# GpSimd makes a slot's last quarter of w2's low parts, and attention's end runs the early table's product and the logits in another order

## The chip, the cores and the metric

The kernel runs on one NeuronCore of a Trainium2 chip. The metric is the device time of one execution, in microseconds (us). The engines are TensorE (PE: matrix products and transposes), VectorE (DVE), ScalarE (ACT), GpSimd (POOL) and SyncE (SP), which only issues transfers. Each works through its own list of instructions in order and waits for the others by semaphores. PE has two clock levels, 1.2 and 2.4 GHz; the profile gives the granted clock as a share of the higher one.

## The reference

Three stages follow each other: attention with a local window and 32 global tokens per head, a layer of 8 experts of which each token takes one, and a dense layer with ELU.

```python
s_ll = np.where(abs(pos[:, None] - pos[None, :]) <= 32, scale * q_l @ k_l.T, -1e9)
a_l = softmax(concat([scale * q_l @ k_g.T, s_ll]))
out_l = a_l @ concat([v_g, v_l])            # 4 batches, 8 heads, 512 local rows of 64
out_g = softmax(scale * q_g @ concat([k_g, k_l]).T) @ concat([v_g, v_l])   # 32 global rows
x = concat([out_g, out_l])                   # 2176 rows of 512
...
logits = x @ w_gate                          # 8 experts
e_idx = argmax(logits)
h = maximum(x[mask] @ w1[e], 0)              # 512 -> 1024
out[mask] = gate_w * eom * (h @ w2[e])       # 1024 -> 512
...
h = x @ w_in                                 # 512 -> 2048
g = where(h > 0, h, exp(minimum(h, 0)) - 1)
return g @ w_out                             # 2048 -> 512
```

## The kernel before

Every large product is made of three products of operands that are split into a high and a low part (x = xh + xo, w = wh + wl): high by high, high by low, low by high. ACT casts the raw weights to the high part (L777), and the low part is raw minus high (L778), by DVE or POOL as the caller says. In the names of the trace, r is a raw weight buffer, w1h, w1l, w2h and w2l are the parts, xh and xo those of the gathered rows, hh and ho those of the hidden rows, h, y, t and tp are banks of PSUM, and misc is the bank that the small results of routing share.

**Attention** runs 16 steps, one per batch and pair of heads, in a software pipeline of 17 turns t. The order of the pieces in a turn is the list PLAN, a string of short names: s0 and s1 are the scores of step t+1, e0 and e1 their maxima and exponentials, pt0 and pt1 the transposes of the probabilities of step t, pc0 and pc1 their copies, pv0 and pv1 the products with the values of step t-1, nm the norm of step t-1 (it makes X, and sends it to the DRAM table x_pre). v1 and v2 are four copies on POOL that build vw, the shifted values of step t, which pv0 and pv1 of the next turn read. Routing follows two steps behind: xt transposes X of step t-2, lm makes its logits in misc, la adds them up in lsum (DVE).

Two slots of expert 0 start on the first three batches alone. Their early table is made in turn 15: ea (L625) counts, eb (L643) is twelve small products that give the two columns of row numbers xidx (DVE, L645), and then two gathers of 128 rows each (L748, an indirect transfer that POOL issues) bring the rows from x_pre to xt. In turn 16, xa transposes them (L798, eight transposes) and makes xh (ACT) and xo (DVE).

**The expert stage** goes through slots of 128 rows. In slot s PE makes the first layer of s in two halves (l1, L811), in between the second layer of s-1 in two halves (l2, L831) and transposes. If the expert of slot s+1 is new, the four quarters of its w1 are split in this slot (L918 and L927 in slot()); if that of slot s is new, the four quarters of its w2 are split (L924, L932, L935). Each of these stands under a branch on a register, as do the slots from 17 on, which run only if the slot count asks for it (L956): an engine that leaves the last slot has to finish what it has there, and then raises the semaphores for the slots that it skips. Here 20 of 26 slots run.

**The dense stage** begins behind it: transposes of the first rows (L990), their split (ACT L992, DVE L993) into the buffer that held the raw w2 of odd slots, the conversion of the dense weights (ACT L1011, POOL L1012), the second layer of the last slot (L831 once more), and then the products of the dense layer (L1041, L1099).

The schedule is written by hand; the order of the calls is the order on each engine. Waits follow from the data and from buffers that are used again, banks of PSUM among them: moe() takes banks that attention has left, in the order in which it asks for them.

Of the kernel before, what the change touches and what calls it, by code (L numbers as in the profile page):

```python
# [44 lines left out]
PLAN = (  # L45
    ("pv0 pv1 pt0 s0 lt pc0 xa e0 rg xt rg2 pt1 gt gu gc gd pump v1 pc1 s1 w1 e1 ld gs lm gpv v2 nm rk bq ea ge "
     "gn eb la", "VAVAVV"),
    ("w1 pv0 ld pt0 s0 rg2 lt xt pv1 pc0 pt1 gt v1 pump gu pc1 rk rg s1 gc gd gs v2 e0 lm nm ea e1 xa gpv ge bq "
     "gn eb la", "AAAAAA"),
    ("pv0 ld pt0 rg2 xt pump ea pv1 pc0 pt1 v1 pc1 v2 lm eb nm la", "AAAAAA"),  # L50
    ("pv0 pv1 nm rg2 xt xa lm la", "AAAAAA"),
)


# [71 lines left out]
class Kern:  # L126
# [7 lines left out]
    def new(self, shape, dt, tag, bufs=1):  # L134
        return (self.home.get(tag) or self.main).tile(shape, dt, tag=tag, name=tag, bufs=bufs)
# [5 lines left out]
    def attention(self):  # L141
        nc, tc, I = self.nc, self.tc, self.i
# [209 lines left out]
        def fetch(t):  # L352
            load_kq(t + 4)
            load_v(t + VB - 1 if t else 16)
            if 3 <= t < 11:
                j, h = divmod(t - 3, 2)
                c = slice(512 * h, 512 * h + 512)
                nc.sync.dma_start(out=self.r1[0][:, j, c], in_=self.w1v[0][:, j, c])
            elif 12 <= t < 16:
                h, j = divmod(t - 12, 2)  # L360
                c = slice(2 * j, 2 * j + 2)
                nc.sync.dma_start(out=self.r2[0][:, h, c], in_=self.w2v[0][:, h, c])
# [7 lines left out]
        for t in range(17):  # L370
# [44 lines left out]
                steps["gs"] = lambda: gscores(g0)  # L415
                steps["ge"] = lambda: gexp(g0)
            steps["ld"] = lambda: fetch(t)
            self.plan = PLAN[0 if t < 2 else 1 if t < 15 else t - 13]
            for x in self.plan[0].split():
                if x in steps:  # L420
                    steps[x]()
# [358 lines left out]
    def split_w1(self, s, h, js=(0, 2)):  # L780
        if s < NSLOT:
            c = slice(512 * h, 512 * h + 512)
            for j in js:
                e = self.nc.gpsimd if (h == (1 if s else 0) and j == 2) else self.nc.vector
                self.split(self.w1h[:, j:j + 2, c], self.w1l[:, j:j + 2, c], self.r1[s % 2][:, j:j + 2, c], e)

    def split_w2(self, s, h, js=(0, 2), engines=None):
# [51 lines left out]
    def moe(self):  # L839
        nc, tc, I = self.nc, self.tc, self.i  # L840
        new = self.new
        SP = mybir.EngineType.SP
        self.hps, self.yps, self.tps = ([self.psum(f"{a}{i}") for i in range(n)] for a, n in (("h", 3), ("y", 1), ("t", 3)))
        self.w2h, self.w2l = (new([128, 2, 4, 512], F32R, a) for a in ("w2h", "w2l"))
        self.r1.append(new([128, 4, 1024], F32, "r11"))
        self.r2.append(new([128, 2, 4, 512], F32, "r21"))
# [68 lines left out]
        def slot(s):  # L915
            n0, n1 = self.nw, self.anew(s + 1)
            l1(s, 0)
            with self.when(n1):  # L918
                self.split_w1(s + 1, 0)
            l2(s - 1, 0)  # L920
            trh(s, 0)
            trx(s + 1)
            self.load_x(s + 4)
            with self.when(n0):  # L924
                self.split_w2(s, 0)
            l1(s, 1)
            with self.when(n1):  # L927
                self.split_w1(s + 1, 1)
            self.load_w1(s + 3)
            l2(s - 1, 1)  # L930
            nc.vector.tensor_copy(self.cur, self.scol[:, s % 3])
            with self.when(n0):  # L932
                self.split_w2(s, 1, (0,), (nc.gpsimd,))
            trh(s, 1)
            with self.when(n0):  # L935
                self.split_w2(s, 1, (2,), (nc.vector,))
            self.load_w2(s + 2)
            self.nw = n1

# [287 lines left out]
```

## Time and profile before

| what | value |
|---|---|
| median of 3 runs | 788.71 us (787.2 to 792.68) |
| the profiled execution | 791.05 us, of which the span from the first to the last instruction is 788.7 us |
| mean granted clock of PE | 0.989 |
| attention | 0 to 129 us |
| expert stage | 129 to 384 us |
| dense stage | 384 to 789 us |

The order of time gives an instruction's start and duration (or of several that follow each other, with their count), and in square brackets how long its engine had been idle before it, and what ended that.

### The profile page before, as it was taken

The page shows a single profiled execution, that of the slowest core. Times are in us where ns is not written, and L with a number is a line of the kernel's source. Part 1 is how long each engine was busy: PE and PEld are TensorE (multiplying, and loading weights), DVE is VectorE, ACT ScalarE, POOL GpSimd, SP SyncE. Part 2 cuts the span into 40 slices and gives each one's busy share as a digit, 9 for nine tenths or more (in the row PEclk, how much of TensorE's full clock was granted, in tenths as well). Part 3 has the DMA queues.
Part 4 walks back from the last instruction along what each step waited for, and adds up shares of the span by engine and source line. Part 5 has one row for each costly group of instructions (what it writes and reads, how often), then busy time and mean ns, then how long its engine had stood idle before and what let it go on. Part 6 is the DMA issues. An engine that isn't in the chain of part 4 may idle for free.

```text
span 788.7 us, 15371 instructions
## 1 busy us (share of the span) xinstructions
PE 761.2 (97%) x5550; PEld 626.5 (79%) x5550; DVE 502.0 (64%) x1174; ACT 399.0 (51%) x769; POOL 256.5 (33%) x235
## 2 busy tenths in 40 slices
PE   8999977999999999999799999999999999999996
PEld 6877765888888888888688777888888888999895
DVE  5675774547576779954679999545445454454563
ACT  5767863345456367524567665433344333433442
POOL 5757661314235142711668883200001000200000
PEclk9999998999999999999899999999999999999999
DMA  9878642375665878464332320100001000100000
GB/s 328 250 208 285 183 113 60 102 267 195 214 234 177 301 248 318 142 215 148 98 107 94 110 105 1 67 22 21 0 28 54 0 1 1 54 1 1 27 15 27
DMA packets 42595, 95.09 MB, mean 121 GB/s; under 512 B 7624, under 2 KB 24520, under 8 KB 39816
## 3 DMA queue, kind: packets, MB, share of 16 engines
q1 hardware_dynamic: 39224, 83.17, 31.2%
q0 software_dynamic: 3280, 10.80, 4.3%
q8 instruction: 45, 0.74, 0.4%
q14 instruction: 46, 0.38, 0.2%
HBM read 79.73 MB, written 14.23 MB: 119 GB/s over the span
## 4 chain that ended last, share of the span: by engine, by line
PE 28%; issue 11%; DVE 7%; DMA 3%; ACT 2%; POOL 1%; POOLq 0%; ACTq 0%; DVEq 0%
PE h L1041 14%; PE y L1099 6%; PE t L1099 6%; DVE xo L1073 2%; DVE wo L733 1%; DMA out_dram<-o,oidx 1%; DVE wo L730 1%; DMA out_dram<-raw,oidx 1%; PE t L990 1%; PE y L831 1%; DVE wo L732 1%; DVE r L993 0%; DVE wo L731 0%; DVE xh L1075 0%; ACT r L1011 0%
## 5 line engine op out<-in xcount | busy, mean ns | idle before, releaser
L1041 PE MATMUL h<-r,r 128*128 128x512 f32 (+2 forms) x640 | 178.1, 363 | 0.0
L1041 PEld LDWEIGHTS h<-r,r 128*128 128x128 f32 x640 | 115.2, 188 | 19.2
L1055 ACT ACTIVATE xo<-xh 128x512 f32<-128x512 f32 (+2 forms) x78 | 44.6, 572 | 164.9 <-DVE xh L1053 164.4
L1053 DVE TENSOR_SCALAR xh<-h 128x512 f32<-128x512 f32 (+2 forms) x62 | 37.0, 597 | 81.1 <-PE h L1041 80.2
L748 POOL DMA_INDIRECT xt<-x_pre,xidx x24 | 32.2, 1342 | 168.4 <-POOLq L924 92.9
L811 PE MATMUL h<-w1h,xh 128*128 128x512 f32 x160 | 67.5, 422 | 0.8 <-DVE xo L801 0.8
L831 PE MATMUL y<-w2l,hh 128*128 128x512 f32 x160 | 63.7, 398 | 0.2 <-POOLq L927 0.2
L811 PE MATMUL h<-w1h,xo 128*128 128x512 f32 x160 | 63.6, 398 | 0.0
L831 PE MATMUL y<-w2h,hh 128*128 128x512 f32 x160 | 63.5, 397 | 0.0
L831 PE MATMUL y<-w2h,ho 128*128 128x512 f32 x160 | 63.3, 395 | 0.0
L811 PE MATMUL h<-w1l,xh 128*128 128x512 f32 x160 | 63.0, 394 | 0.0
L1073 DVE SCALAR_TENSOR_TENSOR xo<-xo,xh 128x512 f32<-128x512 f32 (+2 forms) x78 | 58.4, 749 | 3.5 <-ACT xh L1056 3.5
L1105 POOL DMA_INDIRECT out_dram<-raw,oidx x9 | 9.4, 1043 | 151.7 <-ACT raw L1104 136.5
L1041 PE MATMUL h<-r,w1h 128*128 128x512 f32 (+2 forms) x160 | 57.5, 359 | 0.0
L1041 PE MATMUL h<-r,w1l 128*128 128x512 f32 (+2 forms) x160 | 57.5, 359 | 0.0
L823 ACT CAST hh<-t 128x512 fp32r<-128x512 f32 x40 | 23.5, 587 | 61.1 <-PE t L822 57.8
L813 ACT ACTIVATE hs<-h 128x512 f32<-128x512 f32 x40 | 24.0, 599 | 54.4 <-PE h L811 54.4
L1075 DVE TENSOR_TENSOR xh<-h,xo 128x512 f32<-128x512 f32 (+2 forms) x78 | 47.9, 614 | 2.2
L1105 POOL DMA_INDIRECT out_dram<-o,oidx x8 | 8.9, 1112 | 123.6 <-ACT o L1104 110.6
L1056 ACT ACTIVATE xh<-xh 128x512 f32<-128x512 f32 (+2 forms) x78 | 44.6, 572 | 2.5
L253 ACT ACTIVATE pp<-sm,mn 128x128 f32<-128x128 f32 x128 | 40.5, 396 | 10.1 <-DVE mn L251 9.8
L778 DVE TENSOR_TENSOR w1l<-r,w1h 128x1024 fp32r<-128x1024 f32 x24 | 29.1, 1235 | 23.1 <-ACT w1h L777 17.4
(296 smaller groups left out, 1886.2 us busy)
## 6 DMA issues: line engine op xcount, KB each, us to landing
r<-in_moe_w SPq DMA_DIRECT2D x14, 2048.0 KB, 7.8
kq<-in_kq SPq DMA_DIRECT2D x15, 688.0 KB, 5.3
raw<-in_moe_w_in SPq DMA_DIRECT2D x16, 512.0 KB
raw<-in_moe_w_out SPq DMA_DIRECT2D x16, 512.0 KB
vt<-in_vv SPq DMA_DIRECT2D x16, 390.0 KB, 6.8
y_c<-ys SPq DMA_DIRECT2D x20, 258.0 KB, 2.5
yt<-y_c SPq DMA_DIRECT2D x16, 258.0 KB, 3.8
x_pre<-X SPq DMA_DIRECT2D x16, 256.0 KB, 4.3
```

What stands on the lines that cost most here:

```text
L253: A.activation(out=P[n][:, a, :], in_=sm[:, c, :], func=AF.Exp, scale=-1.0, bias=MN[n][:, a:a + 1])
L748: self.nc.gpsimd.indirect_dma_start(out=self.xt[s % 3], out_offset=None, in_=self.x_pre[0:rows], bounds_check=rows - 1, oob_is_err=False, ...
L778: eng_lo.tensor_tensor(out=lo, in0=raw, in1=hi.bitcast(F32), op=ALU.subtract)
L811: self.nc.tensor.matmul(out=ps, lhsT=a[:, j, :], rhs=w[:, j, c], start=(j == 0 and i == 0), stop=(j == 3 and i == 2))
L831: nc.tensor.matmul(out=yp, lhsT=a[:, h, j, :], rhs=w[:, h, j, :], start=(h == 0 and j == 0 and i == 0), stop=(h == 1 and j == 3 and i == 2))
L1041: nc.tensor.matmul(out=ps, lhsT=w, rhs=y[:, k, 0:n], start=(k == 0 and i == 0), stop=(k == 3 and i == 2))
L1053: V.tensor_scalar(out=m, in0=ps, scalar1=0.0, scalar2=None, op0=ALU.min)
L1055: nc.scalar.activation(out=e, in_=m, func=AF.Exp, scale=sign)
L1056: nc.scalar.activation(out=m, in_=m, func=AF.Tanh, scale=0.5 * sign)
L1073: V.scalar_tensor_tensor(out=e, in0=e, scalar=1.0, in1=m, op0=ALU.add, op1=ALU.mult)
L1075: V.tensor_tensor(out=m, in0=ps, in1=e, op=ALU.max)
L1099: nc.tensor.matmul(out=acc[ch, i], lhsT=g[:, c], rhs=w, start=(f == 0 and q == 0), stop=(f == 15 and q == 2))
```

## The change

Four edits. First, the last quarter of a new expert's w2 goes from DVE to POOL, and in exchange the quarter of w1 that POOL made in every slot but the first goes to DVE (split_w1). Second, turn 14 has a plan of its own, in which la comes before ea and e1 in place of last. Third, in turn 15 eb comes right behind pv1, ahead of pc0, pt1, v1 and v2, and in turn 16 lm and la come ahead of xa. Fourth, moe() asks for its PSUM banks in another order: the t banks now take those of tp, and the h banks those that scores and outputs left.

```diff
--- before.py
+++ after.py
@@ -47,8 +47,10 @@
      "gn eb la", "VAVAVV"),
     ("w1 pv0 ld pt0 s0 rg2 lt xt pv1 pc0 pt1 gt v1 pump gu pc1 rk rg s1 gc gd gs v2 e0 lm nm ea e1 xa gpv ge bq "
      "gn eb la", "AAAAAA"),
-    ("pv0 ld pt0 rg2 xt pump ea pv1 pc0 pt1 v1 pc1 v2 lm eb nm la", "AAAAAA"),
-    ("pv0 pv1 nm rg2 xt xa lm la", "AAAAAA"),
+    ("w1 pv0 ld pt0 s0 rg2 lt xt pv1 pc0 pt1 gt v1 pump gu pc1 rk rg s1 gc gd gs v2 e0 lm nm la ea e1 xa gpv ge bq "
+     "gn eb", "AAAAAA"),
+    ("pv0 ld pt0 rg2 xt pump ea pv1 eb pc0 pt1 v1 pc1 v2 lm nm la", "AAAAAA"),
+    ("pv0 pv1 nm rg2 xt lm la xa", "AAAAAA"),
 )
 
 
@@ -415,7 +417,7 @@
                 steps["gs"] = lambda: gscores(g0)
                 steps["ge"] = lambda: gexp(g0)
             steps["ld"] = lambda: fetch(t)
-            self.plan = PLAN[0 if t < 2 else 1 if t < 15 else t - 13]
+            self.plan = PLAN[0 if t < 2 else 1 if t < 14 else t - 12]
             for x in self.plan[0].split():
                 if x in steps:
                     steps[x]()
@@ -781,7 +783,7 @@
         if s < NSLOT:
             c = slice(512 * h, 512 * h + 512)
             for j in js:
-                e = self.nc.gpsimd if (h == (1 if s else 0) and j == 2) else self.nc.vector
+                e = self.nc.gpsimd if (s == 0 and h == 0 and j == 2) else self.nc.vector
                 self.split(self.w1h[:, j:j + 2, c], self.w1l[:, j:j + 2, c], self.r1[s % 2][:, j:j + 2, c], e)
 
     def split_w2(self, s, h, js=(0, 2), engines=None):
@@ -840,7 +842,7 @@
         nc, tc, I = self.nc, self.tc, self.i
         new = self.new
         SP = mybir.EngineType.SP
-        self.hps, self.yps, self.tps = ([self.psum(f"{a}{i}") for i in range(n)] for a, n in (("h", 3), ("y", 1), ("t", 3)))
+        self.tps, self.yps, self.hps = ([self.psum(f"{a}{i}") for i in range(n)] for a, n in (("t", 3), ("y", 1), ("h", 3)))
         self.w2h, self.w2l = (new([128, 2, 4, 512], F32R, a) for a in ("w2h", "w2l"))
         self.r1.append(new([128, 4, 1024], F32, "r11"))
         self.r2.append(new([128, 2, 4, 512], F32, "r21"))
@@ -933,7 +935,7 @@
                 self.split_w2(s, 1, (0,), (nc.gpsimd,))
             trh(s, 1)
             with self.when(n0):
-                self.split_w2(s, 1, (2,), (nc.vector,))
+                self.split_w2(s, 1, (2,), (nc.gpsimd,))
             self.load_w2(s + 2)
             self.nw = n1
 
```

POOL at attention's end, in turn 15 (vw is what pv0 and pv1 of turn 16 read; DMASW0 and DMASW1 are the semaphores of the two gathers' landing). Before:

```order
L180 COPY vw<-vt 128x650 [waits DMAHW7_49,PE_49,Pool_49]
L183 COPY vw<-vt 32x650 [waits Pool_49]
L182 COPY vw<-vt 64x650
L183 COPY vw<-vt 64x650
L748 DMA xt<-x_pre,xidx 128x516 [waits DMAHW1_49,DMAHW4_49,DMAHW0_49,DMAHW6_49,DVE_49,Pool_49]
L748 DMA xt<-x_pre,xidx 128x516
```

and after (the lines are two further down):

```order
L750 DMA xt<-x_pre,xidx 128x516 [waits DMAHW4_49,DMAHW1_49,DMAHW6_49,DMAHW0_49,DMAHW7_49,DVE_49,Pool_49]
L750 DMA xt<-x_pre,xidx 128x516
L182 COPY vw<-vt 128x650 [waits DMAHW7_49,PE_49]
L185 COPY vw<-vt 32x650 [waits Pool_49]
L184 COPY vw<-vt 64x650 [waits DMASW1_49,DMASW0_49]
L185 COPY vw<-vt 64x650
```

The gathers have moved ahead of the four copies, and the third copy waits for both to land.

PE from turn 16 into the first expert products (xT are the transposes of X and of the gathered rows). Before:

```order
L480 MATMUL xT<-ident,X 128x128 x4
L798 MATMUL xT<-ident,xt 128x128 [waits DMASW0_49]
L798 MATMUL xT<-ident,xt 128x128 [waits DMASW1_49,PE_49]
L490 MATMUL misc<-xT,wl 32x128 [waits DVE_49,Activation_49]
L811 MATMUL h_2693<-w1h,xh_74 128x512 [waits DVE_49]
L811 MATMUL h_2693<-w1l,xh_74 128x512
L811 MATMUL h_2693<-w1h,xo_76 128x512
```

and after:

```order
L482 MATMUL xT<-ident,X 128x128 x4
L492 MATMUL misc<-xT,wl 32x128 [waits DVE_49,Activation_49]
L800 MATMUL xT<-ident,xt 128x128 [waits DMASW0_49]
L800 MATMUL xT<-ident,xt 128x128 [waits DMASW1_49,PE_49]
L813 MATMUL h_2697<-w1h,xh_74 128x512 [waits Activation_49]
L813 MATMUL h_2697<-w1l,xh_74 128x512
L813 MATMUL h_2697<-w1h,xo_76 128x512 [waits DVE_49]
```

The logits (L490) stand ahead of the gathered rows' transposes now, and the first expert product waits for ACT's xh, and no longer for DVE's second xo, which read the bank that it used to take.

DVE in the second half of a slot, from the split of the next slot's w1 on. Before:

```order
L927 COMPARE_AND_BRANCH
L778 TENSOR_TENSOR w1l<-r_2702,w1h 128x2x512 [waits DMAHW2_49,DMAHW6_49,PE_49,Activation_49]
L834 TENSOR_SCALAR ys<-y_3003,cur 128x512 [waits DMAHW5_49,PE_49]
L824 TENSOR_TENSOR ho<-t_2699,hh 128x512 [waits Activation_49]
L935 COMPARE_AND_BRANCH
L778 TENSOR_TENSOR w2l<-r_64,w2h 128x1024 [waits DMAHW3_49,DMAHW0_49,Activation_49]
```

and after:

```order
L929 COMPARE_AND_BRANCH
L780 TENSOR_TENSOR w1l<-r_2702,w1h 128x2x512 [waits DMAHW2_49,DMAHW6_49,PE_49,Activation_49]
L780 TENSOR_TENSOR w1l<-r_2702,w1h 128x2x512 [waits PE_49,Activation_49]
L836 TENSOR_SCALAR ys<-y_3003,cur 128x512 [waits DMAHW5_49,PE_49]
L826 TENSOR_TENSOR ho<-t_2695,hh 128x512 [waits Activation_49]
L937 COMPARE_AND_BRANCH
```

DVE has a second quarter of w1 there and none of w2; the quarter of w2 stands on POOL under the same branch, behind the one that POOL made before.

## Rows read from the trace of the kernel before

**Rows 1.** The page's first part: busy time, share of the span, instructions.

```profile
PE 761.2 (97%) x5550; PEld 626.5 (79%) x5550; DVE 502.0 (64%) x1174; ACT 399.0 (51%) x769; POOL 256.5 (33%) x235
```

**Rows 2.** PE's waits, whole run: total us, times, longest us.

```profile
PE t L990 <- DVEq L956: 5.5, 1, 5.5
PE xT L798 <- DMA xt<-x_pre,xidx: 2.6, 1, 2.6
...
PE y L831 <- POOLq L927: 0.2, 1, 0.2
```

**Rows 3.** POOL in order of time at attention's end: start, us, instruction.

```profile
109.73 0.72 POOL L180 COPY vw<-vt 128x650 f32<-128x650 f32 x1 [0.72 <-POOL vw L183]
...
112.08 0.72 POOL L183 COPY vw<-vt 64x650 f32<-64x650 f32 x1
120.65 1.23 POOL L748 DMA_INDIRECT xt<-x_pre,xidx  x1 [7.85 <-DVE X L291]
122.19 1.00 POOL L748 DMA_INDIRECT xt<-x_pre,xidx  x1 [0.31 <-issue]
```

**Rows 4.** DVE and ACT in order of time, same place.

```profile
119.60 0.16 DVE L645 TENSOR_SCALAR xidx<-misc 128x2 int32<-128x2 f32 x1 [1.22 <-PE misc L643]
...
123.31 0.59 ACT L482 COPY xT<-xT 128x512 f32<-128x512 f32 x1 [0.91 <-PE xT L480]
```

**Rows 5.** PE in order of time, from turn 15 to the first expert product.

```profile
118.17 0.66 PE L263 MATMUL pT<-ident,pp 128*128 128x128 f32 x4
...
119.11 0.45 PE L643 MATMUL misc<-Ae,BT 128*128 128x2 f16 x12
120.74 0.22 PE L280 MATMUL o<-vt,pt 128*32 128x65 f32 x1 [1.18 <-DVE X L291]
...
125.86 1.92 PE L798 MATMUL xT<-ident,xt 128*128 128x128 f32 x8 [2.64 <-DMA xt<-x_pre,xidx]
...
129.17 0.80 PE L811 MATMUL h<-w1h,xh 128*128 128x512 f32 x1 [0.81 <-DVE xo L801]
```

**Rows 6.** The gathers' landing: 112 to 135 us (median), and 112 to 160 us.

```profile
xt<-x_pre,xidx POOLq DMA_INDIRECT x2, 4.8
...
DMA to landing us min/median/max: 3.4/4.3/5.2
```

**Rows 7.** Stretches of 1 us: busy us by engine, granted clock, DMA share, GB/s.

```profile
126.00:127.00 1.00, 1.00 (x6) 0.80 (x7) 0.01 (x1) 0.12 (x1) 0.00 (x0) 0.59 0.51 153
133.00:134.00 1.00, 1.00 (x5) 0.82 (x5) 0.00 (x0) 0.59 (x1) 0.00 (x0) 1.00 0.00 0
...
382.00:383.00 1.00, 0.00 (x0) 0.00 (x0) 1.00 (x1) 0.00 (x0) 0.05 (x1) 0.59 0.00 0
389.00:390.00 1.00, 1.00 (x6) 0.82 (x5) 0.53 (x1) 1.00 (x4) 0.76 (x2) 1.00 0.99 326
```

**Rows 8.** DVE and POOL in order of time: a gather beside a quarter of w2.

```profile
145.32 1.23 DVE L778 TENSOR_TENSOR w2l<-r,w2h 128x1024 fp32r<-128x1024 f32 x1
145.37 2.05 POOL L748 DMA_INDIRECT xt<-x_pre,xidx  x1 [0.30 <-issue]
```

**Rows 9.** The way out of the expert stage in order of time.

```profile
379.70 2.35 POOL L778 TENSOR_TENSOR w2l<-r,w2h 128x1024 fp32r<-128x1024 f32 x1 [0.49 <-ACT hh L823]
380.67 2.46 DVE L778 TENSOR_TENSOR w2l<-r,w2h 128x1024 fp32r<-128x1024 f32 x1 [0.22 <-ACT w2h L777]
384.51 2.82 PE L990 MATMUL t<-ident,yt 128*128 128x128 f32 x12 [5.49 <-DVEq L956]
385.78 1.32 ACT L992 CAST r<-t 128x512 fp32r<-128x512 f32 x2 [5.14 <-PE t L990]
...
388.41 0.63 PE L831 MATMUL y<-w2l,hh 128*128 128x512 f32 x1
389.24 0.75 POOL L1012 TENSOR_TENSOR w1h<-win,r 128x256 fp32r<-128x256 f32 x1 [7.19 <-ACT r L1011]
...
394.05 0.63 PE L1041 MATMUL h<-r,r 128*128 128x512 f32 x2
```

## The prediction

> **What bounds the kernel now.** Three views were read: the page's first part for the balance of the engines, the list of who waited for whom on TensorE (PE), and the order of time around each long wait in it. PE is busy for 97% of the span [rows 1], so only what it waits for, and what it runs at half clock, can be won or lost. Its list has one wait of 5.5 us, at the first transposes behind the expert stage (L990, for VectorE, DVE), and one of 2.6 us, at the first transposes of gathered rows (L798); inside the expert slots the longest is 0.2 us, for GpSimd (POOL) [rows 2]. Each long wait ends with the granted clock at 0.50, the lower of the two levels: it fell in 126 to 127 us and was back at 133, and fell again in 382 to 383 and was back at 389 [rows 7]. So the change is worth what it does at attention's end, near 120 us, and at the way out of the expert stage, near 384 us.
>
> **Inside the slots: nothing.** POOL makes three quarters per new expert before and after; one of w1's goes to DVE and one of w2's comes. A quarter takes DVE 1.23 us beside little POOL work and POOL 2.35 [rows 8, 9]. DVE then has two w1 quarters behind each other; the following slot needs them only in its second half. PE's longest wait there being 0.2 us [rows 2], the term is 0, with bounds of -0.2 and +0.5 us. The cover is the rest of a slot; if it were gone, each new expert could cost up to the 1.1 us by which POOL is slower.
>
> **Attention's end: where the vw copies go.** The four copies that build vw for the last step of attention ran from 109.73 to 112.80 us, 0.72 us each, and POOL was then idle until the gather at 120.65 [rows 3]. Now both gathers stand ahead of them, and the third copy waits besides for both gathers to land (the order shows this wait). The last two products of probabilities and values, which started at 120.74 [rows 5], need all four.
>
> How early does the table come? Its twelve products started at 119.11 behind the transposes at 118.17 and a step of logits; these two now stand behind [rows 5]. That is 0.9 us, and up to 1.3 since the copy of the logits that held the step before it also goes earlier. So the index, made on DVE at 119.60, comes near 118.5 [rows 4]. The gather followed it by 1.05 us and the second by another 1.54 [rows 3, 4]: 119.6 and 121.1. They landed 4.8 us after their issue here, and 3.4 to 5.2 in the whole stretch [rows 6], so the second lands at 124.5 to 126.3; I take 125.5. Two copies with their gaps are 1.5 us [rows 3]: the products can run at 127.0 (126.0 to 127.8) in place of 120.74.
>
> What hangs on them: from 120.74 to the end of the copy of the transposed rows at 123.90 (0.59 us from 123.31) are 3.2 us [rows 4, 5], none of it waiting for the gather. Then come the logits, now ahead of the gathered rows' transposes (0.4 us), and the eight transposes, 1.92 us at half clock [rows 5], which by then wait for nothing. The first expert product follows them at once: its bank is another one, so that the 0.81 us for the second xo goes [rows 5]. Together 127.0 + 3.2 + 0.4 + 1.9 = 132.5 us, against 129.17: +3.3 us. At full clock the transposes take half as long, and with the early end of the range this is +1.4; with the late end and half clock already in the products it is +5.
>
> Then the clock. Before, the expert products ran at half clock from 129.17 to about 133 [rows 5, 7], which cost half of that, 1.9 us. PE will have done nearly nothing from about 119.5 to 127, a longer pause than either that ended in half clock [rows 2], so I count on half clock here too. If full clock is back near 133, as before, the products lose only 0.3 us to it and 1.6 come back; if it stays until 136, nothing does. I take +2.5 us for this place, with bounds of 0 and +4.5.
>
> The pull of the earlier gather is therefore lost: the wait of 2.6 us goes [rows 2], and what is late next is the vw copies.
>
> One rule is to be weighed here. A gather that ran beside a DVE quarter took POOL 2.05 us, where the two here took 1.23 and 1.00 [rows 3, 8]. The Trainium skill (SBUF — State Buffer, "SBUF: two separate sides") says that DVE and GpSimd share a port pair as an exclusive lock, and that a GpSimd-issued DMA cannot write its descriptors while DVE holds it. By that rule the earlier gathers could meet other DVE work and take 2.05 each, which would make this place about 1.9 us dearer; by the rows here they keep 1.23 and 1.00. It returns as a rival.
>
> **The way out of the expert stage.** PE's first transposes there wait for DVE to leave the last slot. DVE's last work in it is the w2 quarter of 380.67 to 383.13 (2.46 us beside POOL's), and PE started 1.38 us behind its end [rows 9]. This quarter now goes to POOL, so DVE can leave before 380.67 and PE start at 382.05 or sooner: -2.5 us for the transposes. But two things behind them wait for POOL: ScalarE's (ACT) copies of these transposes, which overwrite the buffer that the split reads, and the second product of the last slot's second layer. POOL's earlier quarter ends at 382.05; another of 2.35 us ends at 384.4, and with the same 1.38 us POOL is out at 385.8; I allow up to 386.8, as POOL has more waits on its way. ACT's copies began at 385.78 [rows 9], so they gain nothing and stay close to where they were; so does POOL's first piece of the dense stage at 389.24, and PE does not need it before 391. The product of 388.41 can run at 385.8 to 386.8: -1.6 to -2.6 us. From it to the first dense product at 394.05 are 5.6 us, of which about 0.3 are the last of the half clock that ended near 389 [rows 7, 9]; at full clock throughout the first dense product comes at 391.1, -2.9 us, and with the late end and half clock until 390 at about 393.6, -0.4. PE's pause is now split in two (379.0 to 382, and from the transposes' end to POOL's release), so I do not count on full clock. I take -1.6, with bounds of -0.4 and -2.9. In the dense stage the first chunk hangs on PE's first products, so the gain carries on.
>
> **The sum.** +2.5 - 1.6 + 0 = +0.9 us. The profiled execution took 791.05 us with a span of 788.7, and it is 2.3 us above the median of the runs shown, 788.71; the sum is 791.95 in that execution and 789.6 against the median. That is forecast as no change.
>
> **The rivals.**
> (a) Faster: the landing wait is already over when POOL comes to it. Then the four copies follow the second gather with their 3.07 us (121.1 + 1.0 + 3.1 = 125.2), 1.8 us before my 127.0, and attention's end costs +0.7, or gives 1.5 if full clock is back early; with the exit at full clock (-2.9) the sum is -2.2 to -4.4: near 785.5. For it speaks that gathers here landed in as little as 3.4 us [rows 6]; against it, that the two in question needed 4.8.
> (b) Slower than before: the gathers are stretched on POOL by DVE work. If both take the 2.05 us of [rows 8], 1.9 us more than here, the vw copies end near 128.9, and attention's end costs +4.4. The point from which this decides is 127.4 us for the end of the last copy: later than that, the loss exceeds even the exit's whole gain of 2.9. With an exit of -0.4 to -1.6 the sum is +2.8 to +4: 791.5 to 792.7. For it: the 2.05 us row [rows 8]. Against it: DVE has mostly short instructions here.
> (c) The change does not do what it says at the exit: POOL's way out is so long that it holds PE as long as DVE did. Then the exit gives 0 and the sum is +2.5: 791.2. For it: both engines were in the slot until 382 to 383 [rows 9]. Against it: PE's transposes no longer stand behind POOL.
>
> **How the numbers follow.** Forecast 0.55, (a) 0.20, (b) 0.15, (c) 0.10. The likeliest case gives 789.6 us. The bounds of the sum are 0 - 2.9 = -2.9 and 4.5 - 0.4 = +4.1; with (a) below and (b) above the range is 785.5 to 793.5, which also covers the 5 us by which the three runs differ. About 1%, 7.9 us, is what a measurement of this kernel can tell from no change. No case reaches that: the two long waits are 8.1 us together [rows 2], and neither goes whole. So faster by over 1% has 0.03, within 1% 0.94, slower by over 1% 0.03.
>
> **What would show it.** Right: the gather's start near 119.6 us, the third vw copy only after 124, PE waiting 4 to 7 us for POOL ahead of the last products of attention, no wait for the gather at the transposes, the first expert product near 131 to 133; at the exit, PE's wait for DVE cut to about 3 us with a second one for POOL at the second-layer product. Wrong: vw copies that end before 125, clock at full level through either place, or a wait of PE in the slots above 0.5 us.

## The result

The changed kernel takes 797.39 us (median of 4 runs, 795.84 to 798.32) where the kernel before takes 787.96 us: a ratio of 1.0109 with a 95% interval of 1.0086 to 1.0132, that is 6.8 to 10.4 us more. The forecast was 789.6 us, no change. The profiled execution of the changed kernel took 797.98 us with a span of 796.2, against 791.05 and 788.7.

Where the 7.5 us of span went is read by putting the same milestones of TensorE beside each other in the two traces (us from the start of the span):

| milestone | before | after | difference | lost since the one above |
|---|---|---|---|---|
| early table's second set of products (L690, now L692) | 141.39 | 143.35 | +1.96 | +1.96 |
| transposes of hs in the last slot (L822, now L824) | 378.40 | 382.28 | +3.88 | +1.92 |
| first transposes of yt (L990, now L992) | 384.51 | 391.35 | +6.84 | +2.96 |
| first dense product (L1041, now L1043) | 394.05 | 401.44 | +7.39 | +0.55 |
| end of the span | 788.7 | 796.2 | +7.5 | +0.1 |

Attention's end lost about what was forecast (+2.5). The two other places did not: the slots lost 1.9 us, and the exit 3.0 to the transposes and 3.5 to the first dense product, where nothing and a gain of 1.6 stood in the sum. Lines of the changed kernel stand two below those of before.

TensorE's waits over the whole run of the changed kernel (total us, times, longest us), which answer to [rows 2]:

```profile
PE t L992 <- DVEq L958: 8.4, 1, 8.4
PE o L282 <- POOL vw L185: 7.2, 4, 3.8
...
PE y L833 <- DVE ho L826: 0.3, 1, 0.3
PE y L833 <- POOL w2l L780: 0.3, 1, 0.3
```

The wait for the gathered rows is gone, and one for the vw copies has come, as forecast. The wait at the exit, which was to shrink from 5.5 us, is 8.4, and it still names VectorE (DVE).

**Attention's end.** GpSimd (POOL) and PE there in order of time (start, us, instruction), which answer to [rows 3, 5]:

```profile
117.82 1.24 POOL L750 DMA_INDIRECT xt<-x_pre,xidx  x1 [8.97 <-DVE X L293]
119.36 1.00 POOL L750 DMA_INDIRECT xt<-x_pre,xidx  x1 [0.31 <-issue]
120.37 0.73 POOL L182 COPY vw<-vt 128x650 f32<-128x650 f32 x1
...
123.07 0.73 POOL L184 COPY vw<-vt 64x650 f32<-64x650 f32 x1 [1.19 <-DMA xt<-x_pre,xidx]
...
121.93 0.43 PE L282 MATMUL o<-vw,pt 128*32 128x65 f32 x2 [3.76 <-POOL vw L185]
124.63 0.31 PE L282 MATMUL o<-vw,pt 128*32 128x65 f32 x1 [2.27 <-POOL vw L185]
...
131.82 0.79 PE L813 MATMUL h<-w1h,xh 128*128 128x512 f32 x1
```

The gathers are earlier, the copies stand behind them, the third waits for the landing, and PE waits twice for them. The granted clock in stretches of 1 us (busy us by engine, clock, DMA share, GB/s), as in [rows 7]:

```profile
119.00:120.00 1.00, 0.00 (x0) 0.00 (x0) 0.00 (x0) 0.00 (x0) 0.69 (x2) 1.00 0.86 253
121.00:122.00 1.00, 0.07 (x1) 0.07 (x2) 0.00 (x0) 0.00 (x0) 0.82 (x2) 0.50 0.70 173
...
133.00:134.00 1.00, 1.00 (x4) 0.80 (x3) 0.75 (x2) 1.00 (x2) 0.00 (x0) 0.50 0.00 0
135.00:136.00 1.00, 1.00 (x6) 0.80 (x5) 0.95 (x1) 0.59 (x1) 0.00 (x0) 1.00 0.00 0
```

PE was idle from 118.2 to 121.9 us, was granted the lower of its two levels (0.50, 1.2 GHz) from 121 on, and had the upper one back at 135.

**The exit.** DVE, POOL, PE and ScalarE (ACT) in order of time, which answer to [rows 9]:

```profile
382.48 0.75 DVE L836 TENSOR_SCALAR ys<-y,cur 128x512 f32<-128x512 f32 x1 [2.71 <-PE y L833]
383.15 4.54 DVE L837 COPY ys<-cur 128x4 f32<-128x4 f32 x1
...
388.02 0.69 DVE L826 TENSOR_TENSOR ho<-t,hh 128x512 fp32r<-128x512 f32 x1
...
380.67 6.99 POOL L780 TENSOR_TENSOR w2l<-r,w2h 128x1024 fp32r<-128x1024 f32 x3
...
391.35 2.82 PE L992 MATMUL t<-ident,yt 128*128 128x128 f32 x12 [8.44 <-DVEq L958]
...
392.62 1.32 ACT L994 CAST r<-t 128x512 fp32r<-128x512 f32 x2 [8.10 <-PE t L992]
```

The last slot's copy of four columns per partition into the tail of ys takes 4.54 us where its median is 0.16. It ends at 387.69, and POOL's three quarters, one row here because nothing lies between them, end at 387.66. The copy was held until the last of them was done, and ho and DVE's way out of the slots with it. The same is seen in the slots. Two engines where the hold is longest:

```profile
333.48 7.14 DVE L837 COPY ys<-cur 128x4 f32<-128x4 f32 x1
...
333.50 7.09 POOL L780 TENSOR_TENSOR w2l<-r,w2h 128x1024 fp32r<-128x1024 f32 x3
```

A copy of 0.16 us takes 7.14, as long as the three quarters. Four other slots have it at 4.63 us and hide it. Around 318 us, where two slots with new experts follow each other, one operation of DVE after the other is held:

```profile
323.05 1.69 DVE L837 COPY ys<-cur 128x4 f32<-128x4 f32 x1
324.78 2.33 DVE L933 COPY cur<-scol 128x4 f32<-128x4 f32 x1
...
321.35 3.37 POOL L780 TENSOR_TENSOR w2l<-r,w2h 128x1024 fp32r<-128x1024 f32 x1
324.68 2.40 POOL L780 TENSOR_TENSOR w2l<-r,w2h 128x1024 fp32r<-128x1024 f32 x1
...
327.75 0.50 PE L833 MATMUL y<-w2h,ho 128*128 128x512 f32 x1 [0.27 <-DVE ho L826]
```

The first of these copies ends with POOL's second quarter (324.7 us) although the third follows without a gap, so a waiting copy comes in between two quarters at some places and not at others. PE stops at five places between 327 and 346 us. Four of them (327.75, 331.51, 341.69 and 345.45 us, 0.1 to 0.3 us each) stand behind DVE's held work, and each moves the milestones behind it by 0.4 to 0.5 us: that is the 1.9 us. The fifth, at 335.96 us for POOL's first quarter, has its like in the kernel before (0.2 us) [rows 2].

### The profile page after: what moved, and what is told of

It reads as the page before. It is cut to its first block, busy times and chain, and to the rows that moved or that the text cites. A ratio compares the mean times of both kernels' runs of the same rounds, so it can differ in the third digit from the quotient of the medians.

```text
span 796.2 us, 15348 instructions
## 1 busy us (share of the span) xinstructions
PE 764.1 (96%) x5550; PEld 627.9 (79%) x5550; DVE 510.3 (64%) x1174; ACT 398.8 (50%) x769; POOL 255.9 (32%) x235
## 4 chain that ended last, share of the span: by engine, by line
PE 30%; issue 11%; DVE 6%; DMA 1%; ACT 1%; POOL 1%; POOLq 0%; ACTq 0%
PE h L1043 14%; PE y L1101 7%; PE t L1101 7%; DVE xo L1075 2%; DVE wo L735 1%; DVE wo L732 1%; DMA out_dram<-raw,oidx 1%; PE t L992 1%; PE y L833 1%; DVE wo L734 1%; DVE r L995 0%; DVE wo L733 0%; DMA out_dram<-o,oidx 0%; ACT r L994 0%; ACT r L1013 0%
## 5 line engine op out<-in xcount | busy, mean ns | idle before, releaser
L1043 PE MATMUL h<-r,r 128*128 128x512 f32 (+2 forms) x640 | 178.1, 363 | 0.0
L1043 PEld LDWEIGHTS h<-r,r 128*128 128x128 f32 x640 | 115.2, 188 | 19.2
L1043 PE MATMUL h<-r,w1h 128*128 128x512 f32 (+2 forms) x160 | 57.5, 359 | 0.0
L1043 PE MATMUL h<-r,w1l 128*128 128x512 f32 (+2 forms) x160 | 57.5, 359 | 0.0
L780 POOL TENSOR_TENSOR w2l<-r,w2h 128x1024 fp32r<-128x1024 f32 x22 | 53.2, 2447 | 0.2
L780 DVE TENSOR_TENSOR w1l<-r,w1h 128x1024 fp32r<-128x1024 f32 x31 | 39.2, 1302 | 21.6 <-ACT w1h L779 20.9
```

Of the source, the lines that this page charges most:

```text
L780: eng_lo.tensor_tensor(out=lo, in0=raw, in1=hi.bitcast(F32), op=ALU.subtract)
L1043: nc.tensor.matmul(out=ps, lhsT=w, rhs=y[:, k, 0:n], start=(k == 0 and i == 0), stop=(k == 3 and i == 2))
```

## The experiments

Theory A: POOL's three quarters of w2 follow each other without a gap, and DVE's small copies are held until the last is done; that makes the slots and the exit late. Rivals: B, POOL's third quarter is itself too late, and the held copies only lie beside it; C, the loss comes from the two edits together, by the later start of the expert stage. A ratio without "of" is to the kernel before, runs of the same chip.

**1. The exchange of quarters alone (e1_swap).**

```diff
-                e = self.nc.gpsimd if (h == (1 if s else 0) and j == 2) else self.nc.vector
+                e = self.nc.gpsimd if (s == 0 and h == 0 and j == 2) else self.nc.vector
...
-                self.split_w2(s, 1, (2,), (nc.vector,))
+                self.split_w2(s, 1, (2,), (nc.gpsimd,))
```

> Only the exchange of the two quarters between GpSimd and VectorE; the plan and the PSUM order stay those of before. Theory A (the 128x4 copies on VectorE are held until GpSimd's run of three quarters ends: 4.54 us at the exit in the changed kernel's trace, 7.14 us at worst in a slot): the late slots lose their 1.9 us and the exit its 3.0 us here too, so 5 to 6 us over before (ratio 1.006 to 1.008), with TensorE's wait at the exit at 8.4 us. Theory C (the loss comes from the two edits together, by the later start of the expert stage): under 2 us, ratio under 1.0025, and a wait at the exit near 5.5 us.

Measured: 793.28 against 788.95 us, ratio 1.0055 (1.0038 to 1.0073). The exit wait is 8.4 us, the copy there 4.54, and from L690's products to the last transposes of hs the slots take 238.91 us, 1.9 more than before. C falls; the exchange alone loses at both places. The ratio is a little under what theory A gave (1.006 to 1.008): from the exit's transposes to the first dense product this trace takes 8.97 us, 0.6 less than the kernel before.

**2. The order edits alone (e2_order)**: the plan and the PSUM order of the change, the quarters as before.

```diff
-    ("pv0 ld pt0 rg2 xt pump ea pv1 pc0 pt1 v1 pc1 v2 lm eb nm la", "AAAAAA"),
-    ("pv0 pv1 nm rg2 xt xa lm la", "AAAAAA"),
...
+    ("pv0 ld pt0 rg2 xt pump ea pv1 eb pc0 pt1 v1 pc1 v2 lm nm la", "AAAAAA"),
+    ("pv0 pv1 nm rg2 xt lm la xa", "AAAAAA"),
...
```

> Only the plan of attention's end and the PSUM order; the quarters stay where they were before. Theory A: the expert stage begins about 2.0 us later (measured 1.96 us in the changed kernel), the slots and the exit stay as before (wait at the exit 5.5 us), so +2 us, ratio 1.002 to 1.003. Theory C: the exit grows here too, +5 us or more.

Measured: 791.97 us, ratio 1.0040 (1.0025 to 1.0055), +3.2 us, a little more than expected. The exit wait is 5.6 us and the slots take 237.03 us, as before. The two edits add, within their intervals: 0.55 and 0.40% beside 1.09% for both. POOL in order of time, and PE's list of waits (100 to 420 us):

```profile
123.10 0.73 POOL L184 COPY vw<-vt 64x650 f32<-64x650 f32 x1 [1.95 <-DMA xt<-x_pre,xidx]
```

```profile
PE o L282 <- POOL vw L185: 6.8, 2, 3.7
PE t L992 <- DVEq L958: 5.6, 1, 5.6
```

**3. The changed kernel with the small copies on ScalarE (e3_actcopy).**

```diff
-            nc.vector.tensor_copy(self.ys[:, DM:XROW], self.cur)
+            nc.scalar.copy(out=self.ys[:, DM:XROW], in_=self.cur)
...
-            nc.vector.tensor_copy(self.cur, self.scol[:, s % 3])
...
             trh(s, 1)
+            nc.scalar.copy(out=self.cur, in_=self.scol[:, s % 3])
```

> The changed kernel with the two 128x4 copies of a slot (the tail of ys, and cur) on ScalarE, the copy of cur behind the cast of hh. Theory A: VectorE's last operation in the final slot ends some 4.5 us earlier, the exit's wait falls from 8.4 to 3.5 to 5 us, the 1.9 us of the late slots go, and what is left over before is attention's 2 us less about 1 us: -0.5 to +1.5 us, ratio 0.9995 to 1.002. Theory B (GpSimd's third quarter itself, out only at 387.7 us, holds the exit, and the held copies only lie beside it): the wait stays over 7.5 us, and the time stays 5 us or more over before.

Measured: 792.32 us, ratio 1.0042 (1.0020 to 1.0064): with the copies out of DVE's way, the time is that of the order edits alone (1.0040). The exit wait is 4.9 us, though POOL's three quarters are all there, 380.08 to 387.07. B, which gave over 7.5 us, falls as the main cause. That PE starts here just behind POOL's last quarter does not save it: in run 6 PE starts at 382.90 us, with POOL's quarters running to 386.42. In order of time, DVE's last operation in the slots, and two of PE's waits:

```profile
383.02 0.69 DVE L826 TENSOR_TENSOR ho<-t,hh 128x512 fp32r<-128x512 f32 x1 [0.33 <-ACT hh L825]
```

```profile
PE t L992 <- DVEq L958: 4.9, 1, 4.9
PE t L824 <- ACTq L920: 1.2, 1, 1.2
```

The time is above what theory A gave (0.9995 to 1.002) for two reasons: a new wait of 1.2 us for ACT in the slots, and an exit that gained only 0.6 us between the last transposes of hs and those of yt (5.49 against 6.11). DVE's ho ended at 383.71 and PE started at 387.23, 3.5 us later, where the prediction counted 1.38. This second gap is taken up in runs 7 and 9.

**4. The control: the kernel before with the copies on ScalarE (e4_actcopy_before)**, the same diff on the kernel before.

> The kernel before with the same two copies on ScalarE: the control for the run above. Theories A and B: there the copies are held too (1.68 to 2.46 us in six of the slots), but not where TensorE waits for them, so no change: within 0.5 us, wait at the exit 5.5 us. If moving the copies alone gives 2 us or more, the run above says less about GpSimd's third quarter.

Measured: 787.48 us, ratio 0.9979 (0.9961 to 0.9996); 1.7 us less (0.3 to 3.1), a little more than expected. In its trace the slots take 236.52 us against 237.01, since PE's one stop there is gone; the exit wait is 5.7 us, and the span, 788.6 us against 788.7, shows nothing of the rest. Where POOL has no run of three, moving the copies is worth 0.2%; on the changed kernel (1.0109 to 1.0042) it was worth three times that.

**5. The order edits with the vw copies ahead of the early table (e5_copies_first).**

```diff
-    ("pv0 ld pt0 rg2 xt pump ea pv1 eb pc0 pt1 v1 pc1 v2 lm nm la", "AAAAAA"),
+    ("pv0 ld pt0 rg2 xt pump v1 v2 ea pv1 eb pc0 pt1 pc1 lm nm la", "AAAAAA"),
```

> The order edits alone, with the last turn's four vw copies put ahead of the early table instead of behind it; no exchange of quarters. If attention's end lost its time because GpSimd's copies stand behind the two gathers and the third one waits for them to land (1.95 us of waiting in the trace of the order edits alone, TensorE 6.8 us for vw), the wait of TensorE for vw is gone, the first expert product comes at or before the 129.17 us of the kernel before, and the time is that of before or up to 1.5 us under it: ratio 0.998 to 1.001. If the early table itself or the logits ahead of the gathered rows cost the time, it stays 2 to 3 us over before, ratio near 1.003.

Measured: 787.15 against 790.75 us, ratio 0.9953 (0.9935 to 0.9971), better than expected: from +0.40% to -0.47% by the place of four copies. They run at 108.45 to 111.5 us, ahead of the gathers at 118.75 and 120.28; PE's last waits for vw at attention's end are gone, one of 2.0 us for the gathered rows is back, and the first expert product comes at 126.22 us:

```profile
124.47 1.93 PE L800 MATMUL xT<-ident,xt 128*128 128x128 f32 x8 [1.99 <-DMA xt<-x_pre,xidx]
126.22 0.79 PE L813 MATMUL h<-w1h,xh 128*128 128x512 f32 x1
```

So neither the earlier table nor the earlier logits cost anything; the copies behind the gathers did.

**6. w2's last quarter on GpSimd, and nothing given back (e6_w2_only).**

```diff
-                self.split_w2(s, 1, (2,), (nc.vector,))
+                self.split_w2(s, 1, (2,), (nc.gpsimd,))
```

> The kernel before with w2's last quarter on GpSimd and nothing given back: w1's quarter stays on GpSimd too. Theory A (GpSimd's unbroken run of three quarters holds the 128x4 copies): the run of three is there, now with w1's quarter ahead of it in the same slot, so the late slots and the exit lose as in the exchange: exit wait 8.0 to 9.0 us, ratio 1.005 to 1.010. If instead VectorE's extra quarter of w1 made it late, the exit stays near 5.5 us and the ratio under 1.002.

Measured: 787.69 against 790.75 us, ratio 0.9956 (0.9941 to 0.9972): faster, against theory A as it stood. POOL and DVE at the exit:

```profile
378.86 2.41 POOL L778 TENSOR_TENSOR w2l<-r,w2h 128x1024 fp32r<-128x1024 f32 x1
381.75 4.67 POOL L778 TENSOR_TENSOR w2l<-r,w2h 128x1024 fp32r<-128x1024 f32 x2 [0.49 <-ACT hh L823]
...
381.32 0.16 DVE L835 COPY ys<-cur 128x4 f32<-128x4 f32 x1
...
382.90 1.50 PE L990 MATMUL t<-ident,yt 128*128 128x128 f32 x12 [1.81 <-DVEq L956]
```

The three quarters are there, but with a gap of 0.49 us between the first and the second, and the copy passes in it, in 0.16 us. What makes the gap is read from the line of w1's block (L927, skipped in this slot since no new expert follows), whose sequencer rows are, here and in the changed kernel:

```profile
L927 POOLq COMPARE_BRANCH  x1: 45/45/45, 378.1 to 378.1; - x1
L927 POOLq EVENT_SEMAPHORE  x1: 17/17/17, 381.3 to 381.3; - x1
```

```profile
L929 POOLq COMPARE_BRANCH  x1: 45/45/45, 379.7 to 379.7; - x1
```

Where the block holds an instruction of POOL, skipping it raises POOL's semaphore in its place, and that waits for POOL's work so far: 381.3, the end of the first quarter at 381.27. POOL goes on only behind it, and the second quarter starts at 381.75; ACT's hh, which the row above names, is only what ended last before that. Once w1's quarter had gone to DVE, the block was empty on POOL, nothing waited, and the three quarters closed up. Theory A stands with this addition: it is the half of the exchange that takes work off POOL that removes the gap. In the slots the gap does not save everything: they take 238.30 us here, 1.3 more than before. In the slot around 318 us POOL now has four quarters, w1's among them, and between 322.6 and 327.3 us the last two hold two more operations of DVE (2.1 and 2.5 us, where the same take 0.4 beside no quarter), and PE stops 0.7 us for DVE's xo. The gain of this run is all at the exit.

Second, DVE needed only 0.6 us from its branch out of the slots to the semaphore on which PE waits. The rows of the exit's line (first and last start; the first branch is the one out of the slots) in this kernel, in the one before, and in the changed one:

```profile
L956 DVEq COMPARE_BRANCH  x2: 47/55/63, 382.1 to 382.9; - x2
L956 DVEq EVENT_SEMAPHORE  x2: 21/21/21, 382.7 to 382.8; - x2
```

```profile
L956 DVEq COMPARE_BRANCH  x2: 47/55/63, 380.9 to 384.7; - x2
L956 DVEq EVENT_SEMAPHORE  x2: 21/21/21, 384.4 to 384.6; - x2
```

```profile
L958 DVEq COMPARE_BRANCH  x2: 47/55/63, 388.3 to 391.5; - x2
L958 DVEq EVENT_SEMAPHORE  x2: 21/21/21, 391.3 to 391.4; - x2
```

Before, it branched at 380.9, while its last quarter still had 2.2 us to run, and was out 3.6 us later; in the changed kernel 3.0 us, in run 3 3.9.

**7. The kernel before without DVE's last quarter in the last slot (e7_leave_out).**

```diff
-                self.split_w2(s, 1, (2,), (nc.vector,))
+                if s == 19:
+                    nc.scalar.copy(out=self.w2h[:, 1, 2:4], in_=self.r2[s % 2][:, 1, 2:4])
+                else:
+                    self.split_w2(s, 1, (2,), (nc.vector,))
```

> The kernel before without VectorE's subtraction for w2's last quarter in slot 19, the last that runs here: the low parts of that quarter are left out of the work. No run of three on GpSimd, VectorE's last operation is that of ho, near 379.8 us. By the prediction's step (the way out is 1.4 us from the end of the last operation) TensorE's wait at the exit falls from 5.5 to about 2.5 us. By the other reading (the way out is 3 to 4 us from the branch, which VectorE takes as soon as the last operation is issued, so that the subtraction lay beside it) it falls only by the 0.9 us from 380.67 to 379.76: to 4.3 to 5.0 us, and the time by 0.5 to 1 us.

Measured: 791.76 against 790.75 us, ratio 1.0004 (0.9990 to 1.0019). The exit wait is 5.2 us, hardly less than 5.5 and above the 4.3 to 5.0 expected of the other reading: DVE branches at 380.8, 1.65 us behind the start of the last transposes of hs (2.5 before), and needs 4.1 us. The prediction's step, which gives 2.5 us of waiting, falls. Taking the quarter away altogether gains next to nothing, since it lay beside the way out.

**8. Order edits, copies first, and the small copies on ScalarE (e8_best)**: the diffs of runs 3 and 5 with the quarters as before.

> A version put together from the parts that cost nothing: the order edits with the vw copies ahead of the early table, and the two 128x4 copies of a slot on ScalarE; the quarters stay as before. If both parts carry what they showed alone (the copies on ScalarE 0.9979 of before; the order with the copies first 0.998 to 1.001) the ratio is 0.996 to 0.999; if the early table's order still costs, 1.000 to 1.002.

Measured: 787.51 us, ratio 0.9954 (0.9939 to 0.9970), that of run 5 and just under the range expected: the copies on ScalarE add nothing to it.

**9. Run 6 with its code moved (e9_pad).** A second copy of cur in each slot that runs, and six in slots that don't:

```diff
-            nc.vector.tensor_copy(self.cur, self.scol[:, s % 3])
+            for _ in range(3 if s == 21 else 1 if s == 20 else 2):
+                nc.vector.tensor_copy(self.cur, self.scol[:, s % 3])
```

> The kernel with w2's last quarter on GpSimd and nothing given back, whose exit wait was 1.8 us and whose VectorE needed 0.6 us from its branch out of the slots to its semaphore (3.0 to 4.1 us in all other kernels so far). Added: 18 second copies of cur on VectorE, one in each slot that runs, and 6 in slots that never run, so that VectorE's branch and its target stand at the same places of its code as in the kernel before; nothing else. If the short way out hangs on where the code stands, it is 3 to 4 us again, the exit wait 4 to 5 us, and the time 2.5 to 3.5 us over that kernel's: ratio 0.999 to 1.001. If it hangs on VectorE having no subtraction left to do, or on the hour at which it branches, the way stays under 1 us and the ratio at 0.995 to 0.997.

Measured: 792.44 against 791.05 us, ratio 1.0025 (1.0007 to 1.0042), where run 6 had 0.9956. The copy of ys at the exit is 0.16 us as there, and DVE branches 1.8 us behind the last transposes of hs (1.65 there), but is out only 4.2 us later, and PE waits 5.5 us:

```profile
L957 DVEq COMPARE_BRANCH  x2: 47/55/63, 380.9 to 385.3; - x2
L957 DVEq EVENT_SEMAPHORE  x2: 21/21/21, 385.1 to 385.2; - x2
```

So the short way went with nothing but these copies added: moving the code is enough to lose it. The loss is more than was expected (0.999 to 1.001); its trace takes 790.1 us against 786.1 of run 6, with 3.7 us more at the exit and 0.7 in the slots.

**10. The exchange with 32 columns left on GpSimd (e10_gap).**

```diff
...
+                if s and h and j == 2:
...
+                    self.nc.scalar.copy(out=hi, in_=raw)
+                    for g, k in ((self.nc.vector, slice(0, 480)), (self.nc.gpsimd, slice(480, 512))):
+                        g.tensor_tensor(out=lo[:, :, k], in0=raw[:, :, k], in1=hi[:, :, k].bitcast(F32), op=ALU.subtract)
...
```

> The exchange of the two quarters alone, but with 32 of the 512 columns of w1's last quarter left on GpSimd, so that GpSimd has an instruction in that block again and jumps over it, or runs it, between the first and the second of w2's quarters. If the 128x4 copies are held because GpSimd's three quarters follow one another without a gap (in the kernel with w2's quarter alone there is one of 0.34 to 0.49 us, and the copy of the last slot passes in 0.16 us), the copy at the exit is back to 0.16 us and none is over 2.6 us; VectorE's way out of 3 to 4 us from its branch then gives an exit wait of 4 to 5.5 us, and the ratio is 0.998 to 1.001 where the exchange alone had 1.0055. If the number of quarters on GpSimd decides, and not the gap, the copies stay at 4.5 us, the exit wait at 8.4 us, the ratio at 1.005.

Measured: 790.47 against 791.05 us, ratio 0.9995 (0.9977 to 1.0012), where the exchange without this piece had 1.0055. The gap is back, and with it the copy at the exit:

```profile
378.95 0.16 DVE L841 COPY ys<-cur 128x4 f32<-128x4 f32 x1
...
376.48 2.41 POOL L778 TENSOR_TENSOR w2l<-r,w2h 128x1024 fp32r<-128x1024 f32 x1
379.38 4.65 POOL L778 TENSOR_TENSOR w2l<-r,w2h 128x1024 fp32r<-128x1024 f32 x2 [0.49 <-ACT hh L829]
```

No copy in it takes over 2.46 us; the exit wait is 4.5. POOL does as many quarters of w2 as in run 1: the missing gap was most of the cost. The slots still take 0.7 us more than before (237.73 against 237.01).

**11. What was faster, together (e11_best2)**: the order edits with the copies first (run 5), and w2's last quarter on GpSimd with w1's left there (run 6).

> The two parts that were faster alone, together: the order edits with the vw copies ahead of the early table (0.9953 of before), and w2's last quarter on GpSimd with w1's left there too (0.9956). They touch different stages (attention's end and the exit), so the gains should add: 0.990 to 0.993. If the short way out of VectorE hangs on the code's place, it should stand, since this kernel's slots have the same code; if not, 0.994 to 0.996.

Measured: 784.36 against 791.05 us, ratio 0.9900 (0.9871 to 0.9929), the fastest of all. The exit wait is 1.8 us, the way out 0.6 us as in run 6, the one for the gathered rows 1.6.

**12. The other half of the exchange (e12_w1_only).**

```diff
-                e = self.nc.gpsimd if (h == (1 if s else 0) and j == 2) else self.nc.vector
+                e = self.nc.gpsimd if (s == 0 and h == 0 and j == 2) else self.nc.vector
```

> The other half of the exchange: the kernel before with all of w1's low parts on VectorE, and w2's last quarter left there too. No run of three on GpSimd, so by theory A no 128x4 copy over 2.5 us at the exit and an exit wait of 5 to 6 us; VectorE does one quarter of 1.22 us more in each slot with a new expert, in its idle time: ratio 0.999 to 1.002. If VectorE's extra quarter were what made the exchange slow, 1.004 or more.

Measured: 789.25 against 791.05 us, ratio 0.9971 (0.9954 to 0.9989), a little faster than expected; the exit wait is 4.8 us. Without POOL's piece of w1 its two quarters of w2 close up here too. The copy at the exit comes just behind the end of the first (380.51) and is held for the whole of the second, which ends at 382.81:

```profile
380.60 2.25 DVE L835 COPY ys<-cur 128x4 f32<-128x4 f32 x1
...
378.11 4.70 POOL L778 TENSOR_TENSOR w2l<-r,w2h 128x1024 fp32r<-128x1024 f32 x2
```

DVE's way out takes 1.4 us here (383.6 to 385.0), which makes up for the later branch. Each half of the exchange alone is a little faster than the kernel before; only both together make a run of three without a gap.

## Why the prediction was wrong

**Attention's end: right in its steps, its size in part by luck.** The forecast was +2.5 us with bounds of 0 and +4.5; the profiled execution shows +1.96, the order edits alone +3.2 (2.0 to 4.3). The steps came as put: the gather follows the index by 1.06 us (1.05 forecast), the third copy waits for the landing, PE waits for the copies, the first expert product is 2.65 us later (3.3), and half clock lies on it. But the index came 1.7 us earlier than forecast (116.76 and not 118.5), the rows landed sooner behind it, and the last copy ended at 124.6 and not 127.0, which is one of the prediction's own signs of being wrong (copies that end before 125). From there to the first expert product it took 7.2 us and not the 5.5 counted, of which 3.6 were taken from rows at full clock, since PE was at half clock from 121 on. The two misses nearly cancel. Not all of the last products needed all four copies, as was read: PE ran some at 121.93, behind the second copy. Nor is a microsecond between two traces much: in the eight traces with attention as before, the first expert product comes at 127.8 to 130.1 us. Run 5 shows the cause.

**Rivals (a) and (b): not so.** The landing was not over; the third copy waited 1.19 us for it. The gathers took 1.24 and 1.00 us and not 2.05.

**Inside the slots: a term put at nothing.** Nothing was forecast, with +0.5 us as the worst; it was +1.92. "The cover is the rest of a slot" counted DVE's and POOL's own durations and not that one holds the other. The kernel before had this in its trace: copies of ys of 1.68 to 2.46 us beside POOL's quarters. That DVE's quarter took 2.46 us "beside POOL's" [rows 9] is the same thing. The prediction took it as a price of that quarter alone.

**The way out: the step that failed.** "This quarter now goes to POOL, so DVE can leave before 380.67 and PE start at 382.05 or sooner" gave -2.5 us for the transposes and -1.6 for the whole place; it was +2.96 to the transposes, and +0.55 to the first dense product. Two things in it were wrong.

First, DVE was not free of POOL when its quarter had gone. Its copy of ys met the second of three quarters that had closed up, and was held for 4.54 us (runs 1, 3 and 10). This makes the difference between the exchange and the kernel before.

Second, the 1.38 us behind the end of DVE's quarter are not the way out. That starts at DVE's branch, taken as soon as the last operation is issued, and takes 3.0 to 4.2 us in eleven of the fourteen traces of this study, before and after among them; the quarter's 2.46 us lay beside it. So the quarter could give back no more than the 0.8 us by which the branch comes earlier in run 7, and not 2.5; there the place from the last transposes of hs to those of yt was 0.3 us shorter (5.83 against 6.11). That is why the exchange with its gap put back (run 10) is no faster than before, though its copy passes: it gains 0.9 us at this place and loses 0.7 in the slots.

With both set right, attention's +2.5 would have stood beside a slot and exit stage of about +5, and the sum would have been near 796 us.

**Rival (c)** expected an exit without gain since POOL's way out would hold PE. The exit had no gain, but PE waited for DVE (8.4 us), and ACT's copies of the transposes followed these by the same 1.27 us as before. POOL's own way out held nobody; its quarters held DVE's copy.

**The clock at the exit.** Full clock was not counted on, rightly. PE paused 8.4 us, and the granted clock was at its lower level from 387 until 397:

```profile
385.00:386.00 1.00, 0.00 (x0) 0.00 (x0) 1.00 (x1) 0.00 (x0) 1.00 (x2) 1.00 0.03 8
387.00:388.00 1.00, 0.00 (x0) 0.00 (x0) 0.86 (x2) 0.00 (x0) 0.66 (x1) 0.50 0.00 0
...
396.00:397.00 1.00, 1.00 (x4) 0.71 (x4) 0.48 (x2) 1.00 (x3) 0.97 (x2) 0.50 0.92 227
397.00:398.00 1.00, 1.00 (x6) 0.82 (x5) 0.97 (x2) 1.00 (x5) 1.00 (x2) 0.97 0.96 334
```

That is the 0.55 us between the transposes and the first dense product. The length of the pause alone does not set it: in run 1, behind the same 8.4 us, the clock was back some 3 us behind the first transposes and not 6, and the stretch took 8.97 us against 9.54 before. In run 6, where PE paused 1.8 us, the clock stayed at 1.00 throughout, and the stretch took 8.57 us.

## What to carry to other kernels

When work moves between VectorE and GpSimd, look for the shortest VectorE instructions beside GpSimd's long ones, and at gaps: a copy of 0.16 us can wait for a whole run of GpSimd instructions, and taking one instruction off GpSimd can close the gap that let it pass. An engine's way out of skipped code is counted from its branch and not from the end of its last operation; work still running there may cost nothing, and its removal may give nothing. A transfer that is pulled forward drags what is queued behind its issue into its landing: what needs neither goes ahead of it.

## What the runs showed of the hardware

A VectorE copy of 128x4 fp32 within SBUF (0.16 us) is held by a GpSimd subtraction with both inputs in SBUF: 2.25 us beside one (run 12 at the exit), 4.80 beside two that follow without a gap (run 12 at 331.6 us), 4.54 and 7.14 beside the later two and all of three (the changed kernel), while a gap of 0.49 us lets it through (runs 6 and 10). It is not held to the end of the run everywhere: around 318 us a copy came in where one quarter ended and the next followed at once (it was done at 324.74 us in the changed kernel, at 318.92 in the one before). What decides between the two was not tested. VectorE's operations on PSUM (L836, 0.75 us) and ScalarE's copies (0.20 us at 382.89 in run 3) were not held in the same stretches. The Trainium skill (SBUF — State Buffer, "SBUF: two separate sides") says that VectorE and GpSimd take their shared port pair for whole instructions and that the later one blocks fully. These rows agree, and go further: the wait can be longer than one instruction of the other engine.

VectorE's branch out of the slots took 3.0 to 4.2 us in most kernels, 1.4 in run 12 and 0.6 in runs 6 and 11, and run 6 with 24 short instructions more in its code (run 9) had 4.2 in place of 0.6. The Trainium skill (Runtime: NRT & Kernel Launch, "Instruction fetch mechanics") says that a taken branch whose target lies outside the instructions held has to fetch them first. The numbers agree with it; which part of the code was held in which kernel is not visible in the traces, so this cause is argued and not shown, and the gain of runs 6 and 11 at the exit can go again with any edit that moves VectorE's code.
